# ReLUs and output sums of an MLP placed first by a planner, slack planned for attention and Fourier tasks, and weights loaded between the second batch's pairs

## The chip, the core and the metric

The kernel runs on one core of a Trainium2 chip. Five engines work side by side, each through its own instructions strictly in order: TensorE (PE in the profile; PEld is its weight load), VectorE (DVE), ScalarE (ACT), GpSimd (POOL) and SyncE (SP). SP, ACT and POOL also issue DMA transfers, which run on sixteen DMA engines. An instruction that waits holds up everything behind it on its engine. The metric is the device time of one execution in microseconds (us). The median of three runs of the kernel before is 344.29 us.

## What is computed

```python
def _attn_ref(q, k, v, mem_k, mem_v):            # q, k, v: 4 x 8 heads x 768 x 64
    chunk, left_ctx, right_ctx = (32, 16, 8)     # 8 memory rows per head
    for c in range(nc):
        k_full = concat(mem_k, k[l_start:r_end]); v_full = concat(mem_v, v[l_start:r_end])
        a = softmax(scale * q_c @ k_full.T)
        out[c] = a @ v_full

def _moe_ref(x, w_ch1, w_ch2):                   # x: 4 x 768 x 512, from the heads of out
    u = x + real(fft(fft(x, axis=1), axis=2))
    un = (u - mean(u)) / sqrt(var(u) + 1e-06)    # over the 512 columns
    return u + maximum(un @ w_ch1, 0.0) @ w_ch2  # w_ch1 512 x 2048, w_ch2 2048 x 512
```

All inputs and the output are float32.

## The kernel before

There are four batches. Each goes through three stages.

*Attention.* A batch has eight heads, handled as four pairs. The pairs are numbered 0 to 15 over all batches, so pairs 0 to 3 are batch 0 and pairs 4 to 7 batch 1. For one pair, SP loads Q, K and V (`e_load_q`, `e_load_k`, and `e_load_v` once for each head; tiles `qf`, `kf`, `va`, three buffers each, reused in turn). Q and K are cast to bf16 (`qb`, `kb`, one buffer each): on DVE for batch 0, on POOL for the others. PE turns them (`trq`, `trk`), ACT copies the turned tiles (`qT`, `kTb`). POOL copies a piece of each head's `va` to other partitions (`e_overlap`, L299). PE then makes scores for half of the sequence (`sc`, 12 matmuls), ACT takes the exponential (`e`), PE multiplies with the values (`xa`, 24 matmuls), and DVE divides (L373, L374) into the batch's `xsb`; all this twice a pair. `sc` and `xa` have one PSUM buffer each.

*Fourier part.* DVE folds `xsb` by symmetry (`zy`, `pq`, `ff`), and the result is split into a high and a low half-precision part (`hi` on ACT, `lo` on DVE). This is done for an even and an odd part, called parity 0 and parity 1 here. PE makes the transform along the sequence (`ps`, 60 matmuls a batch), ACT and DVE write it back (`up`, `dn`), PE makes the transform along the columns (`pm`, 48 matmuls a batch, in six column tiles of 8). For each tile DVE adds it into `xsb` and takes mean and variance (L474, L480, L481), ACT writes the centred row (`un`), PE turns it (`tp`), DVE copies it (`unT`). POOL makes one `rstd` a batch when all six tiles have their variance.

*MLP.* Two halves of the sequence. Each has 16 products `ph` of four matmuls (w1), each followed by a ReLU on ACT (`hT`), and then three output tiles `pc` of 16 matmuls (w2). DVE adds each output to `xsb` (`osb`, L534) and ACT issues the store.

*Weights.* `w1_sb` and `w2_sb` are each filled by four DMA transfers that POOL issues (L671, L673); they convert from float32 on the way.

*What sets the order.* All work is added as tasks to `Plan` (L38 to L113), each with an engine, a planned cost, tasks that it follows, buffers that it takes and gives, and a rank. `Plan.order` plays the tasks forward in planned time: whenever an engine is free it takes the task of lowest rank that is ready and finds its buffers free. On SP nothing may overtake: the lowest rank is waited for. The sequence that comes out is the program order of every engine; on the chip only dependencies count, and planned times have no other effect. A `margin` makes a task count as ready only so much after the task on another engine that it follows. Rank is normally the order of adding. MLP tasks have `MLPS` (1000000) added, so that they go after all attention and Fourier tasks that are ready. Tasks with `fill=True` are warming matmuls on zeros with the highest rank; the first `ph` ends them.

```python
mg, mgl = (MARGIN, 3 * MARGIN) if b == 1 else (0.0, 0.0)
...
add("PE", 0.28, lambda: e_warm(5), [t_warm], rank=2 * MLPS, fill=True)
```

Of the kernel before, what the change touches and what calls it, by code (L numbers as in the profile page):

```python
# [34 lines left out]
MARGIN = 0.5  # L35


class Plan:  # L38
# [18 lines left out]
    def order(self):  # L57
# [7 lines left out]
        placed = []  # L65
        while any(waiting.values()):
# [39 lines left out]
            if not moved:  # L106
                times = ([v for v in idle.values() if v > now] + [g[0] for g in gives]
                         + [x for t in placed for x in (t["done"], t["done"] + MARGIN, t["done"] + 3 * MARGIN) if x > now])
# [8 lines left out]
def kernel(  # L117
# [439 lines left out]
    for i in range(NKT):  # L557
        t_clear["kTb", i] = add("POOL", 1.15, lambda i=i: nc.gpsimd.memset(kTb[i], 0.0))
# [9 lines left out]
    for nm, parts, y, r, NN, c in (("S", tabS, yS.rearrange(fl3), rS.rearrange(fl3), S, 1.3),  # L568
                                   ("D", tabD, yD.rearrange(fl2), rD.rearrange(fl2), DM, 0.6)):

        t1 = [add("DVE", 0.5, lambda p_=p_: nc.vector.tensor_scalar(
# [13 lines left out]

    def attention(n):
        b, pr = seq[n]
        lq = add("SP", 0.35, lambda: e_load_q(n), take=("qf",), moved=1.3)
        lk = add("SP", 0.35, lambda: e_load_k(n), [t_clear["kf", n] if n < NS else None],
                 take=("kf",), moved=1.3)  # L590
        lv = [add("SP", 1.1, lambda hh=hh: e_load_v(n, hh),
                  [t_ones[n] if n < NV else None],
                  take=("va",) if hh == 0 else (), moved=1.2) for hh in range(2)]
        first = b == 0
        mg, mgl = (MARGIN, 3 * MARGIN) if b == 1 else (0.0, 0.0)
# [3 lines left out]
        ov = [add("POOL", 0.84, lambda hh=hh: e_overlap(n, hh), [lv[hh]], margin=mgl) for hh in range(2)]  # L599
        behind = kept.get("v0") if b == 1 else None  # L600
        tq = add("PE", 0.40, lambda: e_turn_q(n), [cq, t_idb, behind], take=("tr",), give=("qb",),
                 margin=mg)
# [4 lines left out]
                 margin=mg)  # L607
# [4 lines left out]
        for g in range(2):  # L612
            s_ = add("PE", 0.32, lambda g=g: e_scores(n, g), [eq, ek], take=("sc",),
                     give=("qT", "kTb") if g == 1 else (), margin=mg)
# [5 lines left out]
                     margin=mg)  # L620
# [40 lines left out]
    def e_all_sines():  # L661
# [9 lines left out]
    t_w1 = [add("POOL", 0.7, lambda dt=dt: nc.gpsimd.dma_start(  # L671
        w1_sb[:, dt, :], moe_w_ch1[ts(dt, P), :]), [x_last], moved=3.5) for dt in range(NDT)]
    t_w2 = [add("POOL", 0.7, lambda g=g: nc.gpsimd.dma_start(  # L673
        w2_sb[:, ts(g, 4), :], w2v[:, ts(g, 4), :]), [x_last], moved=3.5) for g in range(4)]


    def fourier(b):
        nrm = [[t_norm[b * HP + i, g] for i in ii for g in range(2)] for ii in ((0, 1), (2, 3))]
# [86 lines left out]

    def RELU(i):
        return MLPS + i
# [46 lines left out]
```

## Time and profile before

| what | value |
|---|---|
| median of three runs (lowest to highest) | 344.29 us (340.43 to 344.6) |
| the profiled execution: its time, its span | 341.38 us, 339.6 us |
| mean granted TensorE clock | 0.967 |
| PE busy | 311.2 us (92%) |
| DVE, ACT, POOL busy | 187.6, 168.3, 81.1 us |
| read from and written to HBM | 28.11 MB, 6.29 MB |

The span runs from the first to the last instruction; 1.8 us of the execution's own time lie outside it. Rows of a timeline give the start, the duration, the engine, the line, the operation, the output and input tiles and a count; a bracket at the end says how long the engine stood idle before the row and what ended that. Rows of the chain of waits give start, duration and a piece of the chain that ended last. In the strips of the page each digit is a tenth of the busy share in one of forty slices of 8.49 us. Matmuls overlap each other, so a group's mean duration is longer than the time from one matmul to the next.

### The profile page before, as it was taken

How to read it: one execution, taken by the hardware profiler on the slowest of the kernel's cores; microseconds unless marked ns; L12 is line 12 of the kernel's file. 1: busy time of each engine (PE TensorE's matmuls, PEld its weight loads, DVE VectorE, ACT ScalarE, POOL GpSimd, SP SyncE). 2: the span in 40 equal slices, each digit the busy share in tenths (PEclk: the TensorE clock that was granted, in tenths of full speed). 3: DMA queues.
4: the chain of work that ended last, by engine and by line, in shares of the span. 5: the costliest groups of instructions: out<-in, count | busy, mean ns of one | idle time of the engine just before them, and what ended most of it. 6: DMA issues, size and time to landing. Idle time of an engine off the chain costs nothing.

```text
span 339.6 us, 7885 instructions
## 1 busy us (share of the span) xinstructions
PE 311.2 (92%) x3339; PEld 210.4 (62%) x3339; DVE 187.6 (55%) x359; ACT 168.3 (50%) x297; POOL 81.1 (24%) x88
## 2 busy tenths in 40 slices
PE   7978976999979999589999997799999999999995
PEld 7867974988656577466665655555645454554542
DVE  8945696289299988988673369860710100101001
ACT  7754873456867466758523723356226053250620
POOL 5333992231975145720001200000010000000000
PEclk9997997799999999969999999799999999999998
DMA  5999999996555065620001200010010100201001
GB/s 137 213 198 181 210 205 234 209 208 128 144 147 147 10 169 131 164 63 0 2 31 65 52 2 1 31 64 0 29 67 0 64 31 0 94 0 62 33 31 62
DMA packets 41890, 30.71 MB, mean 90 GB/s; under 512 B 30080, under 2 KB 32128, under 8 KB 41856
## 3 DMA queue, kind: packets, MB, share of 16 engines
q1 hardware_dynamic: 35424, 19.67, 27.1%
q0 software_dynamic: 2688, 4.19, 6.8%
q10 hardware_dynamic: 3744, 6.36, 5.0%
q8 instruction: 26, 0.43, 0.6%
q14 instruction: 8, 0.07, 0.1%
HBM read 28.11 MB, written 6.29 MB: 101 GB/s over the span
## 4 chain that ended last, share of the span: by engine, by line
PE 73%; DVE 10%; DMA 10%; ACT 4%; SPq 1%; issue 1%; ACTq 0%; POOL 0%; POOLq 0%
PE pc L528 25%; PE ph L514 22%; DMA qf<-in_q_dram 8%; PE pm L468 6%; PE xa L363 6%; PE ps L436 5%; PE warm L386 4%; DMA va<-in_v_dram 2%; DVE ff L413 2%; DVE lo L426 2%; PE tp L493 2%; PE sc L342 1%; DVE pq L404 1%; DVE pq L403 1%; ACT va L235 1%; DVE zy L396 1%
## 5 line engine op out<-in xcount | busy, mean ns | idle before, releaser
L521 ACT ACTIVATE hT<-ph 128x384 f16<-128x384 f32 x128 | 61.1, 492 | 70.9 <-PE ph L514 70.5
L514 PE MATMUL ph<-unT,w_sb 128*128 128x384 f16 x512 | 92.5, 327 | 3.9 <-DVE osb L534 3.2
L528 PE MATMUL pc<-w_sb,hT 128*128 128x512 f16 x384 | 87.3, 379 | 0.0
L514 PEld LDWEIGHTS <-w_sb 128*128 128x128 f16 x512 | 48.4, 97 | 37.7 <-issue 8.6
L534 DVE SCALAR_TENSOR_TENSOR osb<-pc,rstd,xsb 128x512 f32<-128x512 f32 x24 | 17.9, 748 | 84.1 <-PE pc L528 84.1
L528 PEld LDWEIGHTS <-hT 128*128 128x128 f16 x384 | 36.8, 98 | 40.5 <-issue 0.4
L299 POOL COPY va<-va 32x780 f32<-32x780 f32 x32 | 31.9, 1008 | 47.0 <-DMA va<-in_v_dram 35.0
L350 ACT ACTIVATE e<-sc,mbias 128x384 f32<-128x384 f32 x64 | 33.7, 581 | 14.1 <-PE sc L342 13.6
L386 PE MATMUL warm<-zeros 128*128 128x128 bf16 x506 | 38.1, 237 | 1.0 <-DVE zero L208 1.0
L386 PEld LDWEIGHTS <-zeros 128*128 128x128 bf16 x506 | 33.5, 107 | 2.0 <-DVE zero L208 1.0
L363 PE MATMUL xa<-va,e 128*64 128x65 f32 x768 | 30.1, 229 | 2.2 <-DVE xsb L374 2.2
L363 PEld LDWEIGHTS xa<-va,e 128*64 128x64 f32 x768 | 25.6, 140 | 7.6 <-issue 6.0
L486 ACT ACTIVATE un<-xsb,mu_s 128x512 f16<-128x512 f32 x24 | 17.3, 720 | 22.9 <-DVE mu_s L481 19.2
L502 POOL TENSOR_SCALAR rstd<-mu_s 128x6 f32<-128x6 f32 x4 | 1.1, 285 | 99.6 <-DVE osb L534 88.3
L448 ACT CAST up<-ps 128x386 f16<-128x386 f32 x16 | 9.6, 602 | 23.4 <-PE ps L436 23.4
L295 POOL CAST kb<-kf 104x1024 bf16<-104x1024 f32 x12 | 17.4, 1446 | 12.6 <-PE trk L321 8.6
L421 ACT CAST hi<-ff 128x768 f16<-128x768 f32 x16 | 13.2, 832 | 12.8 <-DVE ff L413 12.6
L436 PE MATMUL ps<-cosS,hi 128*128 128x193 f16 (+1 forms) x72 | 15.8, 275 | 3.3 <-DVE ff L413 3.3
L474 DVE TENSOR_TENSOR xsb<-pm,xsb 128x512 f32<-128x512 f32 x24 | 16.2, 674 | 4.3 <-PE pm L468 4.0
L374 DVE TENSOR_TENSOR xsb<-xa,zs 128x384 f32<-128x384 f32 x32 | 17.8, 557 | 1.1
L498 DVE COPY unT<-tp 128x512 f16<-128x512 f16 x24 | 9.9, 419 | 15.1 <-PE ph L514 11.6
L436 PE MATMUL ps<-cosS,lo 128*128 128x193 f16 (+1 forms) x72 | 15.6, 274 | 2.4 <-DVE lo L426 2.4
(93 smaller groups left out, 380.8 us busy)
## 6 DMA issues: line engine op xcount, KB each, us to landing
qf<-in_q_dram SPq DMA_DIRECT2D x16, 384.0 KB
kf<-in_k_dram SPq DMA_DIRECT2D x16, 384.0 KB
out_dram<-osb ACTq DMA_DIRECT2D x24, 256.0 KB
va<-in_v_dram SPq DMA_DIRECT2D x32, 176.0 KB
w_sb<-in_moe_w_ch_dram POOLq DMA_DIRECT2D x8, 512.0 KB, 15.3
va<-in_mem_v_dram SPq DMA_DIRECT2D x32, 24.0 KB
va<-in_v_dram SPq DMA_DIRECT2D x16, 28.0 KB
va<-in_v_dram SPq DMA_DIRECT2D x16, 4.0 KB
```

The source lines that it names most:

```text
L295: eng.tensor_copy(kb_of[n].rearrange(cp_b), kf[n % NS].rearrange(cp_q, j=RB))
L299: nc.gpsimd.tensor_copy(v1[0:32, 1:NB, 0:D + 1], v1[96:128, 0:NT, 0:D + 1])
L350: nc.scalar.activation(e1[:, :, :, ts(half, 32)], sc[:, :, 0:6, ts(half, 32)], AFT.Exp, bias=mbias[:, half:half + 1], scale=1.0 / math.sqr ...
L363: nc.tensor.matmul(xa[64 * half:64 * half + 64, st, hh, 0:65], e1[:, hh, t6, :], v1[:, 6 * g + t6 + 1, 0:65], start=True, stop=True)
L374: nc.vector.tensor_tensor(xs[b][:, 3 * g:3 * g + 3, 2 * pr * D:(2 * pr + 2) * D] .rearrange("p s (h d) -> p s h d", h=2), xa[:, :, :, 0:D] ...
L386: nc.tensor.matmul(warm_of[0], zeros, zeros, start=True, stop=True)
L436: nc.tensor.matmul(out_[:, sp, :], part[:, ab, sp * 3 + st, c0:c1], tab[:, sp, st, :], start=(st == 0 and i == 0), stop=(st == 2 and i == 1))
L468: nc.tensor.matmul(pm[:, par, :], lhs, rhs[:, par, :], start=(im == 0), stop=(im == 3))
L514: nc.tensor.matmul(ph[:, 0:384], w1_sb[:, dt, ts(ht, P)], unT_of[b][:, dt, sh * 384:(sh + 1) * 384], start=(dt == 0), stop=(dt == NDT - 1))
L521: nc.scalar.activation(hT_of[b, sh][:, ht, :], ph_of.pop((b, sh, ht))[:, 0:384], AFT.Relu, bias=0.0, scale=-1.0)
L528: nc.tensor.matmul(pc_of[b, sh, stl], hT_of[b, sh][:, ht, ts(stl, P)], w2_sb[:, ht, :], start=(ht == 0), stop=(ht == NHT - 1))
L534: nc.vector.scalar_tensor_tensor(osb, pc_of.pop((b, sh, stl)), rstd_of[b][:, st:st + 1], xs[b][:, st, :], ALU.mult, ALU.add)
```

## The change

1. *MLP ranks.* ReLU tasks, output sums (`osb`) and output stores get `len(plan.tasks) - MLPS`: they now go before everything else that is ready on ACT and DVE. `ph` and `pc` on PE keep their rank.
2. *Slack.* `SPARE` gives three margins a batch (PE tasks; ACT and DVE tasks; tasks behind a load): none for batch 0, 1.5, 0.7 and 2.0 for batch 1, 1.0, 0.3 and 0.5 for batches 2 and 3. Fourier tasks get them too.
3. *Loads on SP.* New ranks put Q and K of pair n+1 ahead of V of pair n, and the planned issue and transfer costs are larger.
4. *Weights.* w1 is issued behind the V copies of pair 4, w2 behind those of pair 6 (`W1_AT`, `W2_AT`), instead of both once pair 3 has its exponentials.
5. *Warming.* A fill is 6 matmuls planned at 0.8 instead of 5 planned at 0.28. 450 fill matmuls become 234; the 56 at the start stay.
6. *Small.* The memsets of `kTb` clear 32 of every 96 columns, and the planned cost of one table operation on DVE is 0.8 instead of 0.5.

```diff
-        lq = add("SP", 0.35, lambda: e_load_q(n), take=("qf",), moved=1.3)
...
+        lq = add("SP", 0.45, lambda: e_load_q(n), take=("qf",), moved=1.5, rank=10 * n)
+        lk = add("SP", 0.4, lambda: e_load_k(n), [t_clear["kf", n] if n < NS else None],
+                 take=("kf",), moved=1.5, rank=10 * n + 1)
+        lv = [add("SP", 2.1 if hh == 0 else 1.4, lambda hh=hh: e_load_v(n, hh),
+                  [t_ones[n] if n < NV else None], rank=10 * n + 15 + hh,
+                  take=("va",) if hh == 0 else (), moved=1.6) for hh in range(2)]
...
-        mg, mgl = (MARGIN, 3 * MARGIN) if b == 1 else (0.0, 0.0)
+        mgp, mg, mgl = SPARE[b]
...
+    SPARE = [(0.0, 0.0, 0.0), (1.5, 0.7, 2.0)] + [(1.0, 0.3, 0.5)] * (B - 2)
...
+    def load_w1(after):
+        return [add("POOL", 0.7, lambda dt=dt: nc.gpsimd.dma_start(
+            w1_sb[:, dt, :], moe_w_ch1[ts(dt, P), :]), [after], moved=3.2, rank=-1)
+            for dt in range(NDT)]
...
     def fourier(b):
+        def add(engine, cost, emit, after=(), **more):
+            return plan.add(engine, cost, emit, after, margin=SPARE[b][0 if engine == "PE" else 1],
+                            **more)
...
-                                rank=RELU(len(plan.tasks))))
+                                rank=len(plan.tasks) - MLPS))
...
-                          rank=MLPS + len(plan.tasks))
+                          rank=len(plan.tasks) - MLPS)
...
+    W1_AT, W2_AT = (1, 0), (1, 2)
...
+            if (b, i) == W1_AT:
+                t_w1 = load_w1(kept["ov"])
+            if (b, i) == W2_AT:
+                t_w2 = load_w2(kept["ov"])
...
-        add("PE", 0.28, lambda: e_warm(5), [t_warm], rank=2 * MLPS, fill=True)
+        add("PE", 0.8, lambda: e_warm(6), [t_warm], rank=2 * MLPS, fill=True)
```

Three places show the moves. The first is POOL at the start of batch 1. `va` buffers 82, 83 and 84 belong to pairs 3, 4 and 5, and 82 then to pair 6; `kb<-kf_80` and `kb<-kf_81` are pairs 4 and 5, and `kf_79` is pair 6. Before:

```order
L291 CAST qb<-qf_77 96x2x8x64
L295 CAST kb<-kf_80 104x2x8x64
L299 COPY va_83<-va_83 32x12x65
L671 DMA w_sb<-in_moe_w_ch_dram 128x2048 x4
L673 DMA w_sb<-in_moe_w_ch_dram 128x4x512 x4
L299 COPY va_83<-va_83 32x12x65
L291 CAST qb<-qf_78 96x2x8x64
L295 CAST kb<-kf_81 104x2x8x64
```

And after, in the same place on POOL:

```order
L297 COPY va_83<-va_83 32x12x65 x2
L677 DMA w_sb<-in_moe_w_ch_dram 128x2048 x4
L293 CAST kb<-kf_81 104x2x8x64
L297 COPY va_84<-va_84 32x12x65
L289 CAST qb<-qf_76 96x2x8x64
L297 COPY va_84<-va_84 32x12x65
L293 CAST kb<-kf_79 104x2x8x64
L297 COPY va_82<-va_82 32x12x65
L289 CAST qb<-qf_77 96x2x8x64
L297 COPY va_82<-va_82 32x12x65
L682 DMA w_sb<-in_moe_w_ch_dram 128x4x512 x4
L293 CAST kb<-kf_80 104x2x8x64
```

The first four weight transfers moved behind both V copies of pair 4, and the other four behind both V copies of pair 6, ahead of the K cast of pair 7.

The second place is SP at pairs 3 and 4 (`va0` is pair 3's V, `va1` pair 4's; `qf1` and `kf1` are pair 4's Q and K, `qf2` and `kf2` pair 5's). Before:

```order
L280 DMA va0_82<-in_v_dram 64x11x64
L281 DMA va0_82<-in_mem_v_dram 8x12x64
L260 DMA qf1_77<-in_q_dram 96x2x512
L265 DMA kf1_80<-in_k_dram 96x2x512
L278 DMA va1_83<-in_v_dram 8x2x64
L279 DMA va1_83<-in_v_dram 56x2x64
```

And after, on SP:

```order
L278 DMA va0_82<-in_v_dram 64x11x64
L279 DMA va0_82<-in_mem_v_dram 8x12x64
L258 DMA qf2_78<-in_q_dram 96x2x512
L263 DMA kf2_81<-in_k_dram 96x2x512
L276 DMA va1_83<-in_v_dram 8x2x64
L277 DMA va1_83<-in_v_dram 56x2x64
```

Pair 4's V now stands behind pair 5's Q and K.

The third place is PE in the Fourier part of batch 3, where the `ps` matmuls of parity 0 end (the last ones write one row, 1x193). Before:

```order
L436 LDWEIGHTS lo_3500
L436 MATMUL ps_3535<-cosS_105,lo_3500 1x193
L436 LDWEIGHTS hi_3572
L436 MATMUL ps_3579<-cosS_105,hi_3572 128x193
L436 LDWEIGHTS lo_3573
L436 MATMUL ps_3579<-cosS_105,lo_3573 128x193
```

And after, on PE:

```order
L434 LDWEIGHTS hi_3314
L434 MATMUL ps_3371<-cosS_105,hi_3314 1x193
L434 LDWEIGHTS lo_3315
L434 MATMUL ps_3371<-cosS_105,lo_3315 1x193
L512 LDWEIGHTS w1_sb_110
L512 MATMUL ph_3399<-unT_2452,w1_sb_110 128x384
```

Parity 1 followed parity 0 at once; now 28 matmuls of `ph` stand between them.

More of the change, by code (lines that the diff above doesn't have):

```diff
@@ L65, in order @@
         placed = []
+        margins = {0.0} | {t["margin"] for t in self.tasks}
         while any(waiting.values()):
@@ L107, in order @@
                 times = ([v for v in idle.values() if v > now] + [g[0] for g in gives]
-                         + [x for t in placed for x in (t["done"], t["done"] + MARGIN, t["done"] + 3 * MARGIN) if x > now])
+                         + [x for t in placed for x in (t["done"] + m for m in margins) if x > now])
                 assert times, [(t["engine"], t["no"], t["take"]) for ts_ in waiting.values()
@@ L557 @@
     for i in range(NKT):
-        t_clear["kTb", i] = add("POOL", 1.15, lambda i=i: nc.gpsimd.memset(kTb[i], 0.0))
+        t_clear["kTb", i] = add("POOL", 0.5, lambda i=i: nc.gpsimd.memset(
+            kTb[i].rearrange("p (b c) -> p b c", b=NB)[:, :, 64:96], 0.0))
     t_col = add("DVE", 0.6, e_rows_of_ones, [t_id])
```

29 lines of the change are left out of this document (11 added, 18 removed).

## The prediction

> **What bounds the kernel now.** I read the page's strips first, then its groups, then the chain of waits in order of time, and last the timelines of PE, POOL and SP.
>
> ```profile
> span 339.6 us, 7885 instructions
> PE   7978976999979999589999997799999999999995
> PEclk9997997799999999969999999799999999999998
> DMA  5999999996555065620001200010010100201001
> L514 PE MATMUL ph<-unT,w_sb 128*128 128x384 f16 x512 | 92.5, 327 | 3.9 <-DVE osb L534 3.2
> L528 PE MATMUL pc<-w_sb,hT 128*128 128x512 f16 x384 | 87.3, 379 | 0.0
> ```
>
> Two stages show. For nine slices (to about 76 us) the DMA engines are full, and PE is filled up with warming matmuls. After that the DMA engines are mostly idle and PE is full, with weak slices. The boundary is the first `ph`, since only the MLP gives PE more work than the loads allow:
>
> ```profile
> 81.49 0.81 PE L514 MATMUL ph<-unT,w_sb 128*128 128x384 f16 x4
> ```
>
> PE's true work is priced from pieces of the chain at full clock, since group means overlap:
>
> ```profile
> 61.09 0.29 PE sc L342 x12
> 64.82 1.01 PE ps L436 x12
> 70.25 1.75 PE pm L468 x16
> 72.00 0.85 PE xa L363 x24
> 78.70 0.34 PE trq L305 x8
> 80.45 0.33 PE tp L493 x4
> 82.52 0.37 PE trk L321 x8
> 314.71 10.40 PE ph L514 x64
> 325.11 10.37 PE pc L528 x48
> 335.51 0.75 DVE osb L534
> ```
>
> A pair costs 0.34 + 0.37 + 2 x 0.29 + 2 x 0.85 = 3.0 us, four of them 12.0. The Fourier part of a batch is 5 x 1.01 + 3 x 1.75 + 6 x 0.33 = 12.3, its MLP 2 x (10.40 + 10.37) = 41.5. A batch is 65.8, all four 263.2 us.
>
> Ahead of its first `ph`, the program order of before has 8 `trq`, 7 `trk`, 14 `sc`, 13 `xa`, all `ps` and `pm` of batch 0 and 4 of its `tp`: 32.0 us of work, done in 81.5. So 231.2 us remain. From the last `pc` (335.5) to the end of the span are 4.1 us. 339.6 - 81.5 - 231.2 - 4.1 leaves **22.8 us that PE loses after the first `ph`**. Most of it stands where a batch's Fourier part begins:
>
> ```profile
> 100.17 0.92 PE L363 MATMUL xa<-va,e 128*64 128x65 f32 x24 [2.17 <-DVE xsb L374]
> 144.64 0.80 PE L514 MATMUL ph<-unT,w_sb 128*128 128x384 f16 x2 [2.65 <-DVE osb L534]
> 147.21 0.34 PE L436 MATMUL ps<-cosS,lo 128*128 128x193 f16 x1 [0.98 <-DVE lo L426]
> 213.68 0.26 PE L436 MATMUL ps<-cosS,hi 128*128 128x193 f16 x1 [3.25 <-DVE ff L413]
> 140.00:150.00 10.00, 6.19 (x59) 4.44 (x60) 9.97 (x13) 5.96 (x12) 4.55 (x4) 0.66 0.52 136
> 210.00:220.00 10.00, 6.01 (x39) 4.43 (x37) 8.50 (x17) 3.45 (x5) 0.00 (x0) 0.83 0.07 26
> ```
>
> These four waits are 9.05 us. In the two windows the granted clock (third number from the end) was 0.66 and 0.83, so at most 3.4 + 1.7 = 5.1 us went there. Some 8.6 us are small waits and switches of task.
>
> **The change, part by part.**
>
> *Weights.* What they do to the loads before:
>
> ```profile
> 32.49 0.84 SPq L260 DMA_DIRECT2D qf<-in_q_dram  x1
> 38.94 0.75 SPq L260 DMA_DIRECT2D qf<-in_q_dram  x1
> 40.26 4.46 SPq L265 DMA_DIRECT2D kf<-in_k_dram  x1
> 62.12 0.34 SPq L260 DMA_DIRECT2D qf<-in_q_dram  x1
> 38.48 3.04 POOL L673 DMA_DIRECT2D w_sb<-in_moe_w_ch_dram  x4
> 44.33 5.40 POOL L295 CAST kb<-kf 104x1024 bf16<-104x1024 f32 x1
> 68.66 0.83 POOL L299 COPY va<-va 32x780 f32<-32x780 f32 x1 [1.80 <-DMA va<-in_v_dram]
> ```
>
> Pair 5's loads take 6.45 us of SP (32.49 to 38.94). Pair 6's take 23.2, with single issues of 4.46 us, as the eight weight transfers run beside them: 16.7 us of delay, 8.4 for each four. Pair 6's V is complete at 68.66. In the changed order only w1 is ahead of it, but also pair 7's Q and K, half of 6.45: I estimate 68.7 - 8.4 + 3.2 = 63.5 us. Bounds are 60 (w1 all done before) and 72 (no relief).
>
> The first `ph` hangs on two chains. One is batch 0's Fourier part:
>
> ```profile
> 49.79 0.54 PE L321 MATMUL trk<-ident_b,kb 104*128 104x104 bf16 x8 [1.99 <-POOL kb L295]
> 59.73 0.51 PE L305 MATMUL trq<-ident_b,qb 96*128 96x96 bf16 x8 [3.29 <-POOL qb L291]
> 61.31 2.85 PE L386 MATMUL warm<-zeros 128*128 128x128 bf16 x25
> 70.09 0.38 PE L468 MATMUL pm<-cosD,up 128*128 128x256 f16 x2
> ```
>
> Here PE stands 3.29 us before pair 6's `trq`, because its Q comes late; the `ps` of parity 1 are queued behind it, and then 25 warming matmuls hold PE for 2.85 us more. In the changed order Q of pair 6 precedes pair 5's V and the weights, so it has landed. Pair 5's `trk` stays at about 49.8 (its cast of 5.40 us on POOL now follows w1's issue and overlaps the same DVE work). Behind it come 24 `ps`, `sc` and `xa`: 2.0 + 0.3 + 0.85, and the next `trq` starts at 53.5 to 55.5; I take 54.5. From `trq` to the first `pm` were 10.4 us, of which 2.85 was warming; 6 of those matmuls now cost 0.7. `pm` comes at 54.5 + 10.4 - 2.85 + 0.7 = 62.7. From `pm` to `ph` were 11.4 us, a DVE chain that is unchanged: **first `ph` at 74 us**.
>
> The other chain is new: pair 8's `trq` and `trk` stand ahead of the first `ph`, and their casts stand on POOL behind w2's issue.
>
> ```profile
> 71.69 1.04 POOL L295 CAST kb<-kf 104x1024 bf16<-104x1024 f32 x1 [0.32 <-DMA kf<-in_k_dram]
> ```
>
> 63.5 + 0.83 (V copy) + 3.04 (w2's issue) + 3 x 1.04 (casts) + 0.37 (`trk`) = 70.9 us, just under 74. If pair 8's K lands late under w2's transfers, this chain decides; by as much as pair 6 was held up, 8.4 us, it gives 79. w2 itself, 8.4 us from 67, is in long before the first `pc`, which has 64 `ph` (10.4 us) ahead of it.
>
> Ahead of the first `ph` are then 9 `trq`, 9 `trk`, 15 `sc`, 13 `xa`, `ps`, `pm` and 5 `tp`: 33.7 us. 229.5 us remain.
>
> *Slack and MLP ranks.* The wait for `osb` (2.65) goes, since `osb` is first on DVE and the ReLUs first on ACT; the ReLUs push casts and exponentials back by a half us each, which the new slack covers on paper. At batch 3, 28 `ph` (4.5 us) now lie between the two parities, where 3.25 was lost. At batch 2, some 28 us of other PE work stand between the last division and the first `ps`, and about 10 us of DVE work must fit there: 0.98 goes. At batch 1 the filler is 12.6 us for DVE work of about 10 with `osb` added, so I keep the 2.17. Of 9.05 us of waits I keep 2.2 and allow 1.0 for new ones; of the clock's 5.1, two; the small 8.6 fall to 6.3. That is 11.5 us. The bounds are 5 (only small switches) and 22.8 (nothing gained).
>
> *Loads reordered.* Each V lands one Q and K later, 3.2 us, with two pairs of Q and K in hand. Batch 0 is held by PE and ACT steps as much as by V, so nothing there. Queued behind SP's waits for a free Q buffer is now the V of the pair before: a rival below.
>
> *Memset, table cost.* POOL stands idle for 2.58 us after the memsets, so a shorter one gains nothing and one of equal length loses nothing:
>
> ```profile
> 8.42 2.37 POOL L299 COPY va<-va 32x780 f32<-32x780 f32 x2 [2.58 <-DMA va<-in_v_dram]
> ```
>
> *Fewer warming matmuls.* 216 fewer. They filled waits ahead of the first `ph`, except where they stood in the way (counted above). What their absence may cost is the clock:
>
> ```profile
> 33.03 1.85 PE L386 MATMUL warm<-zeros 128*128 128x128 bf16 x30
> 50.00:60.00 10.00, 6.71 (x95) 5.29 (x91) 6.56 (x12) 3.57 (x7) 3.10 (x3) 0.83 1.17 227
> 60.00:70.00 10.00, 10.00 (x169) 9.28 (x167) 4.10 (x10) 5.30 (x9) 2.70 (x3) 0.83 1.13 211
> ```
>
> Thirty at full clock took 1.85 us (62 ns each); 25 after the idle 3.29 us took 2.85 (114 ns), in a window with granted clock 0.83, as the one before it. So idle PE is followed by slow PE. The Trainium skill, "TensorE: Matmul & The Clock Gate", in the part on the HAM clock gate, says that PE falls to half rate after an idle window of about 3.4 us and needs as long a busy one to recover; by that rule, which the trace bears out, the change risks a cold PE. I take no cost beyond the 0.7 above, for the waits ahead of 74 us are for data; the upper end is the cold rival.
>
> **Sum.** 74 + 229.5 + 11.5 + 4.1 = 319.1 us span, and 1.8 outside it (341.38 - 339.6): 320.9 us against a profiled 341.38. The median of the runs, 344.29, is 0.85% above that execution, so the forecast on the median's scale is 323.6, said as 324.
>
> **Rivals** (times on the median's scale).
>
> *The DMA queue only moves its jam.* w2 now floods pair 8's Q and K, and the first `ph` stays at 81.5 us; slack still pays. 81.5 + 229.5 + 11.5 + 5.9 = 328.4, scaled 331. For it: 40.26 shows what weights do to K. Against: Q and K are now queued ahead.
>
> *Slack is planned, not real.* `ph` at 74, but 22.8 stays lost, since new waits replace old: 332.2, scaled 335. For it: the DVE row of 140 to 150 has 9.97 busy of 10, and DVE's work does not shrink.
>
> *Neither*, the change does not do what it says: 81.5 + 229.5 + 22.8 + 5.9 = 339.7, scaled 343.
>
> *Cold PE.* At 114 instead of 62 ns a matmul, the 19 us of PE work between 50 and 74 us (`ps` 5.1, `pm` 5.3, five `xa` 4.3, the small tasks some 4) cost 16 more, 3.4 of them paid already (two windows at 0.83): +12.6, 333.5, scaled 336. The Trainium skill's clock gate would do it this way.
>
> *V behind Q and K: slower.* Every V of pairs 4 to 15 comes 3.2 us later, and PE, strictly in order, stands that long at each `xa`: 12 x 3.2 = 38, 359 us, scaled 362. It makes the kernel over 2% slower once the wait exceeds 27 us in all, 2.3 a pair. For it:
>
> ```profile
> POOL va L299 <- DMA va<-in_v_dram: 35.0, 13, 9.6
> ```
>
> V is what POOL waits for most. Against: PE stood only once before `xa`, for 2.17, and by 90 us the DMA engines are half idle.
>
> **Chances.** Forecast 0.50; jam moves 0.13; slack unreal 0.13; neither 0.09; cold 0.07; slower 0.08. Faster by over 2% means under 337.4; about 2% is what can be told here, as the three runs spread over 1.2%. The first two count as faster, most of the third and half of the fourth: 0.76. Same 0.16, slower 0.08. The range begins at first `ph` 71 with 5 lost (71 + 229.5 + 5 + 5.9 = 311.4, scaled 314) and ends at 338, beyond the cold and slack rivals; outside are "neither", "slower" and a little below.
>
> **What would show it.** First `ph` near 74, and V copies of pair 6 near 63; no SP issue of 4 us between pair 5's and pair 6's Q; waits of PE after the first `ph` of 3 to 5 us in all, none for `osb`; the batch 3 `ps` without a wait. Wrong would be: POOL's casts of pairs 7 and 8 behind w2 later than 72 us with PE idle for them, waits at `xa` of over 2 us a pair, or a granted clock well under 0.9 after 80 us.

## The result, and the profile after

The kernel after the change takes 319.7 us (median; 317.68 to 320.28), the kernel before, run beside it, 344.09 us (340.43 to 344.6). The ratio is 0.930, with a 95% interval of 0.923 to 0.938: 7% faster. The profiled execution of after took 319.55 us with a span of 317.8 us.

The page of after, with the same five lines as shown of before (span; PE, its granted clock and the DMA engines in forty slices, now 7.95 us each; the two MLP groups):

```profile
span 317.8 us, 7448 instructions
PE   7697759899999999999999999999999999999994
PEclk9989796999999999999999999999999999999998
DMA  7999999999981695910130001000100100101001
L512 PE MATMUL ph<-unT,w_sb 128*128 128x384 f16 x512 | 92.1, 325 | 1.3 <-DVE osb L532 0.8
L526 PE MATMUL pc<-w_sb,hT 128*128 128x512 f16 x384 | 88.2, 379 | 0.0
```

From the ninth slice on PE is at 9 until the last, and its granted clock is at 0.9 or more from the eighth. The two groups of MLP matmuls are as long as before to about 1% (92.1 and 88.2 us against 92.5 and 87.3): the work didn't shrink, the gaps did. Ahead of that PE is less busy than before in most slices, as there are fewer warming matmuls.

The boundary, again the first `ph` (timeline of PE, after):

```profile
76.04 1.47 PE L512 MATMUL ph<-unT,w_sb 128*128 128x384 f16 x8
```

What PE waits for from there to the end, by the view of waits cut to that stretch (who waits and for whom: us in all, times, longest). First before, from 82 us:

```profile
PE ps L436 <- DVE ff L413: 3.3, 1, 3.3
PE ph L514 <- DVE osb L534: 3.2, 4, 2.7
PE ps L436 <- DVE lo L426: 2.6, 4, 1.0
PE xa L363 <- DVE xsb L374: 2.2, 1, 2.2
```

Then after, from 76 us, the whole answer:

```profile
PE xa L361 <- DVE xsb L372: 0.9, 2, 0.6
PE ph L512 <- DVE osb L532: 0.8, 4, 0.3
PE ph L512 <- ACT hT L519: 0.3, 1, 0.3
PE xa L361 <- POOL kb L293: 0.3, 1, 0.3
```

The waits for `ff` and `lo` are gone and those for `osb` and `xsb` are small; in all 13.2 us became 2.3.

By the prediction's own division of the span:

| | before | after |
|---|---|---|
| first `ph` at | 81.49 us | 76.04 us |
| PE's true work ahead of it (piece prices of the prediction) | 32.0 | 33.7 |
| true work left | 231.2 | 229.5 |
| lost after the first `ph` | 22.8 | 8.2 |
| behind the last `pc` | 4.1 | 4.1 |

So of 21.8 us of span, 7.2 come from the stage of loads (5.45 earlier, and 1.7 us more work done by then) and 14.6 from PE's losses behind it.

Twelve kernels were run to find which edit bought which part. Each was timed beside the kernel before on the same chip, and the ratios below are to that. For every kernel "first `ph`", "work ahead" and "lost" are worked out from its trace as in the table above; "waits" are the idle times of PE of 0.15 us or more behind the first `ph`.

### The profile page after: what moved, and what is told of

The parts are those of the page before. It is cut to its first block, busy times and chain, and to the rows that moved or that the text cites. A ratio compares the mean times of both kernels' runs of the same rounds, so it can differ in the third digit from the quotient of the medians.

```text
span 317.8 us, 7448 instructions
## 1 busy us (share of the span) xinstructions
PE 297.1 (94%) x3123; PEld 197.0 (62%) x3123; DVE 189.6 (60%) x359; ACT 167.0 (53%) x297; POOL 80.2 (25%) x88
## 4 chain that ended last, share of the span: by engine, by line
PE 68%; DVE 19%; DMA 6%; ACT 2%; SPq 1%; issue 1%; POOL 1%; ACTq 0%; POOLq 0%
PE ph L512 26%; PE pc L526 22%; PE pm L466 6%; PE xa L361 5%; PE ps L434 5%; DMA va<-in_v_dram 4%; DVE zy L394 3%; DVE ff L411 3%; DVE osb L532 2%; DMA qf<-in_q_dram 2%; DVE pq L402 2%; DVE lo L424 2%; PE tp L491 2%; DVE pq L401 2%; PE sc L340 1%; DVE xsb L372 1%
## 5 line engine op out<-in xcount | busy, mean ns | idle before, releaser
L512 PE MATMUL ph<-unT,w_sb 128*128 128x384 f16 x512 | 92.1, 325 | 1.3 <-DVE osb L532 0.8
L526 PE MATMUL pc<-w_sb,hT 128*128 128x512 f16 x384 | 88.2, 379 | 0.0
L297 POOL COPY va<-va 32x780 f32<-32x780 f32 x32 | 35.2, 1106 | 69.5 <-DMA va<-in_v_dram 39.7
L348 ACT ACTIVATE e<-sc,mbias 128x384 f32<-128x384 f32 x64 | 33.7, 580 | 17.8 <-PE sc L340 15.6
L361 PE MATMUL xa<-va,e 128*64 128x65 f32 x768 | 31.4, 231 | 6.8 <-POOL va L297 5.2
L361 PEld LDWEIGHTS xa<-va,e 128*64 128x64 f32 x768 | 26.6, 142 | 13.9 <-POOL va L297 6.0
L384 PE MATMUL warm<-zeros 128*128 128x128 bf16 x290 | 23.8, 240 | 1.0 <-DVE zero L206 1.0
L384 PEld LDWEIGHTS <-zeros 128*128 128x128 bf16 x290 | 20.1, 109 | 1.4 <-DVE zero L206 1.0
L371 DVE RECIPROCAL zs<-xa 128x6 f32<-128x6 f32 x32 | 6.0, 188 | 23.3 <-PE xa L361 23.3
L394 DVE TENSOR_TENSOR zy<-xsb 128x768 f32<-128x768 f32 x16 | 19.5, 1226 | 0.2
L424 DVE TENSOR_TENSOR lo<-ff,hi 128x768 f16<-128x768 f32 x16 | 16.6, 1050 | 0.8 <-ACT hi L419 0.8
L478 DVE BATCH_NORM_STATS2 st<-xsb 128x6 f32<-128x512 f32 x24 | 16.6, 693 | 0.7
L434 PE MATMUL ps<-cosS,hi 128*128 128x193 f16 (+1 forms) x72 | 14.4, 260 | 2.7 <-ACT hi L419 2.7
```

Source lines behind the costliest of these rows:

```text
L297: nc.gpsimd.tensor_copy(v1[0:32, 1:NB, 0:D + 1], v1[96:128, 0:NT, 0:D + 1])
L348: nc.scalar.activation(e1[:, :, :, ts(half, 32)], sc[:, :, 0:6, ts(half, 32)], AFT.Exp, bias=mbias[:, half:half + 1], scale=1.0 / math.sqr ...
L361: nc.tensor.matmul(xa[64 * half:64 * half + 64, st, hh, 0:65], e1[:, hh, t6, :], v1[:, 6 * g + t6 + 1, 0:65], start=True, stop=True)
L384: nc.tensor.matmul(warm_of[0], zeros, zeros, start=True, stop=True)
L394: nc.vector.tensor_tensor(zy_of[b, par][:, :, c0:c0 + P], xb[:, :, c0:c0 + P], xb[:, :, HD + c0:HD + c0 + P], ALU.add if par == 0 else ALU ...
L424: nc.vector.tensor_tensor(lo[:, ab].rearrange(fl), ff_of[b, par][:, ab].rearrange(fl), hi[:, ab].rearrange(fl), ALU.subtract)
```

## Experiments on the weights and the loads

**All weights early, planned anew.** The kernel after, but with both weights issued where before had them, behind pair 3's exponentials. The planner takes the loads into account, so the order of all engines changes too.

```diff
+    t_w1, t_w2 = load_w1(x_last), load_w2(x_last)
     done = {0: fourier(0)}
...
-            if (b, i) == W1_AT:
-                t_w1 = load_w1(kept["ov"])
-            if (b, i) == W2_AT:
-                t_w2 = load_w2(kept["ov"])
```

> The changed kernel with one part undone: all eight weight transfers are issued behind pair 3's exponentials again. Theory A (the weights flooded the loads of pairs 5 and 6, and their split made the first ph earlier): the first ph goes back from 76 to 81 or 82 us, V of pair 6 lands at 70 or later, and PE loses about 8 us afterwards as now; some 325 us. Theory B (Q and K ahead of V is what brought the first ph forward, the weights don't matter): first ph within 1.5 us of 76, 320 us. Theory C (nearly all came from slack and ranks): 320 to 322 us.

Measured: 333.96 us (332.21 to 334.56), ratio 0.972 [0.962, 0.982]. First `ph` at 86.29 with 31.6 us of work ahead of it, 10.5 lost. So the place of the weights matters: the first `ph` came even later than before's 81.49. To part the transfers from the planner, the next two keep an order word for word.

**Only the issue moved, early.** After's program order on every engine, except that the eight weight issues stand on POOL behind pair 3's V copies.

```diff
-        kept["ov"] = ov[-1]
+        kept["ov"] = kept["ov", n] = ov[-1]
...
+        behind_ov = {id(kept["ov", n]): ws for n, ws in {3: t_w1 + t_w2}.items()}
+        weights = {id(w) for w in t_w1 + t_w2}
         for t in plan.order():
+            if id(t) in weights:
+                continue
             t["emit"]()
+            for w in behind_ov.get(id(t), ()):
+                w["emit"]()
```

> The changed kernel's program order on every engine, word for word, except that all eight weight transfers are issued behind the V copies of pair 3 on POOL, near 35 us. Theory A (contention of the transfers): the first ph goes from 76 to 84 to 87 us, as where the planner was told of early weights (86.3), the loss afterwards stays at 8 to 11 us, 328 to 332 us. Theory P (the transfers don't matter, the planner's order around them does): first ph within 2 us of 76 and 319 to 322 us.

Measured: 328.77 us (328.0 to 329.43), ratio 0.963 [0.956, 0.971]. The timelines of this kernel, PE at pair 6's `trq`, the first `pm` and the first `ph`, then POOL ahead of that `trq`:

```profile
59.32 0.82 PE L303 MATMUL trq<-ident_b,qb 96*128 96x96 bf16 x8 [4.64 <-POOL qb L289]
71.07 0.38 PE L466 MATMUL pm<-cosD,up 128*128 128x256 f16 x2
84.66 1.47 PE L512 MATMUL ph<-unT,w_sb 128*128 128x384 f16 x8
57.33 0.83 POOL L297 COPY va<-va 32x780 f32<-32x780 f32 x1 [10.85 <-DMA va<-in_v_dram]
58.23 1.03 POOL L289 CAST qb<-qf 96x1024 bf16<-96x1024 f32 x1
```

and PE's first two of these rows in after (the third is shown above):

```profile
54.79 0.52 PE L303 MATMUL trq<-ident_b,qb 96*128 96x96 bf16 x8
62.76 0.38 PE L466 MATMUL pm<-cosD,up 128*128 128x256 f16 x2
```

With the order unchanged, PE stands 4.64 us for the cast of pair 6's Q, and `pm` and `ph` come 8.3 and 8.6 us later. It isn't Q itself that is late now, as it was in before: SP issues it at 34.60, ahead of the jam. Its cast stands on POOL behind the copy of pair 5's V (the first of the two POOL rows), and that waits 10.85 us for its load; in after the same copy goes at 47.91 and the cast at 49.42. The loss behind the first `ph` is 8.0, as after's 8.2. So 8.6 us hang on the place of the eight issues alone, and all of it ahead of the first `ph`. Against this kernel the one above is another 1.6 us later with 2.1 us less work done, and loses 2.5 us more: about 6 us of its span come with the order that the planner makes when the weights are early.

**Only the issue moved, late.** The converse: before's order word for word, with w1 behind pair 4's V copies and w2 behind pair 6's.

```diff
+        kept["ov", n] = ov[-1]
...
+        behind_ov = {id(kept["ov", n]): ws for n, ws in {4: t_w1, 6: t_w2}.items()}
```

(and the same loop as above).

> The program order of the kernel before on every engine, word for word, except that w1 is issued behind both V copies of pair 4 and w2 behind those of pair 6. Theory A: pair 6's trq comes forward from 59.7 to about 55, the first ph from 81.5 to 74 to 77 us, the 22.8 us lost afterwards stay; 336 to 340 us. Theory P (only a new order can use the earlier loads): first ph at 80 to 82, 342 to 345 us.

Measured: 337.41 us (335.49 to 338.8), ratio 0.987 [0.975, 0.9996]. The timeline of PE of this kernel, at the same places, and a wait at batch 3:

```profile
55.27 0.51 PE L305 MATMUL trq<-ident_b,qb 96*128 96x96 bf16 x8
76.00 0.81 PE L514 MATMUL ph<-unT,w_sb 128*128 128x384 f16 x4
210.17 0.34 PE L436 MATMUL ps<-cosS,hi 128*128 128x193 f16 x1 [3.25 <-DVE ff L413]
```

The wait of 3.29 us before pair 6's `trq` is gone and the first `ph` stands at 76.00, 5.5 us earlier than before: the move alone does that. Behind it nothing improves: the wait of 3.25 us for `ff` is there, and 25.6 us are lost, 2.8 more than in before. Only 0.6 of that are waits; the granted clock is below full for longer (0.89, 0.60, 0.97 and 0.69 in the windows of 10 us from 130, 140, 200 and 210 us: at most 8.5 us in all, against 5.1 in before). So half of the early gain is lost again, and the span falls by 2.7 us. The median falls by 5.5 us, with an interval that only just leaves out no gain.

**V ahead of the next pair's Q and K.** The kernel after with the SP ranks taken out (the larger planned costs stay).

```diff
-        lq = add("SP", 0.45, lambda: e_load_q(n), take=("qf",), moved=1.5, rank=10 * n)
+        lq = add("SP", 0.45, lambda: e_load_q(n), take=("qf",), moved=1.5)
...
-                  take=("kf",), moved=1.5, rank=10 * n + 1)
+                  take=("kf",), moved=1.5)
...
-                  [t_ones[n] if n < NV else None], rank=10 * n + 15 + hh,
+                  [t_ones[n] if n < NV else None],
```

> The changed kernel with one part undone: on SP, V of a pair stands ahead of the next pair's Q and K again (larger planned costs kept). Theory A: pair 6's Q now queues behind pair 5's V under w1's transfers, trq of pair 6 comes at 57 to 60 instead of 54.8 us, first ph 2 to 4 us later, 322 to 324 us. Theory B (this part carries the earlier start): first ph at 81 or later, 325 us or more. If V behind Q and K was a cost, as the slower rival said: 318 us or less.

Measured: 320.51 us (319.39 to 321.83), ratio 0.934 [0.926, 0.942], not to be told from after. The parts differ and cancel: first `ph` at 72.34 with 31.6 us of work ahead (3.7 earlier with 2.1 less done), then 11.8 lost against 8.2. So the rival by which Q and K ahead of V cost 3.2 us at every pair is wrong: no such cost shows, and no gain in the sum either.

## Experiments on the slack and the MLP's ranks

**Old margins.**

```diff
-    SPARE = [(0.0, 0.0, 0.0), (1.5, 0.7, 2.0)] + [(1.0, 0.3, 0.5)] * (B - 2)
+    SPARE = [(0.0, 0.0, 0.0), (0.5, 0.5, 1.5)] + [(0.0, 0.0, 0.0)] * (B - 2)
...
-            return plan.add(engine, cost, emit, after, margin=SPARE[b][0 if engine == "PE" else 1],
+            return plan.add(engine, cost, emit, after, margin=0.0,
```

> The changed kernel with one part undone: the margins are those of before (0.5 and 1.5 for attention of batch 1 alone, none for Fourier tasks). Theory A (slack removes the waits at the starts of Fourier parts): first ph at 76 to 79, then 15 to 20 us lost on PE instead of 8, with waits for DVE of 1 to 3 us at ps of batches 1 to 3; 328 to 333 us. Rival (the MLP ranks removed those waits, slack is unreal): 320 to 322 us.

Measured: 332.19 us (331.52 to 335.36), ratio 0.970 [0.961, 0.979]. PE's timeline, the two largest waits and the first `ph`:

```profile
66.96 0.87 PE L319 MATMUL trk<-ident_b,kb 104*128 104x104 bf16 x8 [6.58 <-POOL kb L293]
83.45 0.81 PE L512 MATMUL ph<-unT,w_sb 128*128 128x384 f16 x4
150.37 0.26 PE L434 MATMUL ps<-cosS,lo 128*128 128x193 f16 x1 [3.04 <-DVE lo L424]
```

and POOL's timeline of the same kernel ahead of the first of them:

```profile
62.81 3.01 POOL L682 DMA_DIRECT2D w_sb<-in_moe_w_ch_dram  x4
65.86 1.04 POOL L293 CAST kb<-kf 104x1024 bf16<-104x1024 f32 x1
```

Here the planner had put a `trk` and, behind it, all `pm` of batch 0 where it believed `kb` to be ready. On the chip POOL reached that cast only behind w2's issue (62.81, 3.01 us), which itself follows V's copies, and PE stood 6.58 us in front of `trk` with the `pm` queued behind. That puts the first `ph` at 83.45, 7.4 us later than in after (0.5 us more work done). Behind it 13.2 us are lost instead of 8.2, with the old kind of wait for `lo`. So planned slack is worth about 12 us here, and more than half of it ahead of the first `ph`, where the expectation had placed almost none: in after the `pm` begin at 62.76 (row above), ahead of that `trk`. That the larger margin for tasks behind a load is the one of the three that does it was not tried.

**Old MLP ranks.** ReLUs, output sums and stores last again, everything else as in after.

```diff
-                                rank=len(plan.tasks) - MLPS))
+                                rank=MLPS + len(plan.tasks)))
```

(and the same for output sums and stores).

> The changed kernel with one part undone: ReLUs, output sums and stores have the high rank of before on ACT and DVE. Theory A (slack did most): one wait for osb of 2 to 3 us comes back and little else, 322 to 324 us. Rival (ranks did most): 10 or more us more lost after the first ph, 330 us or more.

Measured: 335.9 us (334.38 to 336.09), ratio 0.978 [0.970, 0.986]. First `ph` at 77.49, near after's, but 23.0 us lost, as much as before's 22.8. The ranks cost the most of the three parts, though the intervals overlap, and all but 1.5 us of it lies behind the first `ph`. Two more runs part the two kinds of task.

**Only the ReLUs first.**

```diff
-                          rank=len(plan.tasks) - MLPS)
+                          rank=MLPS + len(plan.tasks))
...
-                    rank=len(plan.tasks) - MLPS)
+                    rank=MLPS + len(plan.tasks))
```

(the two tasks are `osb` and the store).

> The changed kernel with only the ReLUs placed first on ACT; output sums and stores have the high rank of before. The run without all MLP ranks lost 23.0 us after its first ph, this change's own kernel 8.2. If the ReLUs did it (PE waited for ACT in ph): 9 to 12 us lost, 320 to 324 us. If the output sums did it (a PSUM buffer of pc is held until osb has run): 18 us or more lost, 330 us or more, with waits for osb.

Measured: 333.59 us (332.08 to 334.52), ratio 0.974 [0.969, 0.979]; first `ph` at 76.0 as in after, 20.8 lost.

**Only the output sums and stores first.**

```diff
-                                rank=len(plan.tasks) - MLPS))
+                                rank=MLPS + len(plan.tasks)))
```

(the task is the ReLU).

> The changed kernel with only output sums and stores placed first; ReLUs have the high rank of before. If the output sums did it: 9 to 12 us lost, 320 to 324 us. If the ReLUs did it: 18 us or more lost, 330 us or more, with waits of PE for hT. If it takes both, each of the two runs comes out near 328.

Measured: 323.21 us (322.19 to 323.81), ratio 0.944 [0.940, 0.949]; first `ph` at 77.27, 9.6 lost.

So the output sums with their stores carry it: from the ratios, 0.044 (some 15 us) come back with them, and 0.014 (some 5 us, the intervals just apart) with the ReLUs.

How an addition on DVE can cost that much is in the traces. `pc` and `ph` share two PSUM buffers (the tile pool has `mlp=2`), and a `pc` buffer comes free only by its `osb`. For the kernel with only the ReLUs first, the view of the tile `pc` (count, shortest/median/longest ns, first and last start) and PE's timeline:

```profile
L526 PE MATMUL pc<-w_sb,hT x384: 376/379/390, 90.7 to 325.8; 128*128 128x512 f16 x192
L532 DVE SCALAR_TENSOR_TENSOR osb<-pc,rstd,xsb x24: 731/751/752, 120.1 to 326.3; 128x512 f32<-128x512 f32 x24
108.30 0.92 PE L361 MATMUL xa<-va,e 128*64 128x65 f32 x24 [1.97 <-DVE xsb L372]
120.90 1.02 PE L526 MATMUL pc<-w_sb,hT 128*128 128x512 f16 x4 [0.87 <-DVE osb L532]
```

and the same view of after:

```profile
L526 PE MATMUL pc<-w_sb,hT x384: 376/379/390, 90.7 to 313.3; 128*128 128x512 f16 x192
L532 DVE SCALAR_TENSOR_TENSOR osb<-pc,rstd,xsb x24: 732/751/752, 98.3 to 313.7; 128x512 f32<-128x512 f32 x24
```

Both begin `pc` at 90.7. In after the first `osb` runs at 98.3; with the old rank it stands on DVE behind the attention and Fourier work of batch 1 until 120.1. The first two `pc` tiles then hold both buffers: the second is done at 104.7, no MLP matmul goes until 120.90, and PE has only tasks of which several themselves wait for DVE. No store stands ahead of this first sum, so here it is the sum's own rank. The windows of the stretch from 105 to 121 us (PE's busy time first; granted clock third from the end), ReLUs only first, then after:

```profile
105.00:121.00 16.00, 11.32 (x174) 9.52 (x172) 14.82 (x27) 6.65 (x11) 4.86 (x4) 0.89 0.16 37
```

```profile
105.00:121.00 16.00, 15.12 (x202) 11.06 (x201) 15.86 (x26) 8.68 (x16) 6.06 (x6) 1.00 0.69 167
```

PE is busy 11.32 us of 16 in the one and 15.12 in the other, while DVE is nearly full in both. The same again at batch 3, in milder form. PE and then DVE, ReLUs only first:

```profile
209.86 0.81 PE L512 MATMUL ph<-unT,w_sb 128*128 128x384 f16 x4 [0.64 <-ACT hT L519]
211.25 0.81 PE L512 MATMUL ph<-unT,w_sb 128*128 128x384 f16 x4 [0.58 <-ACT hT L519]
...
217.35 3.59 PE L512 MATMUL ph<-unT,w_sb 128*128 128x384 f16 x20
```

```profile
214.22 0.74 DVE L532 SCALAR_TENSOR_TENSOR osb<-pc,rstd,xsb 128x512 f32<-128x512 f32 x1
```

The half's last `pc` was done before the first of these `ph`, its `osb` runs at 214.22. In between one buffer is left for `ph`, and with matmul and ReLU in turn there is a product every 1.39 us; once `osb` is through, five run in 3.59 us without a wait (the last row). The waits of 0.15 us or more sum to 11.55 us in this kernel against 2.32 in after, 9.2 of the 12.6 us of lost time between them; the rest is spread over pieces too small to name. Of the 9.2, 2.3 are one wait of a `trq` (at 131.84) for a cast of Q on POOL, which the run with only the sums first has too (2.4) and after hasn't; they are not the sums' work.

**The ranks alone.** The kernel before with only the three ranks changed.

```diff
-                                rank=RELU(len(plan.tasks))))
+                                rank=len(plan.tasks) - MLPS))
...
-                          rank=MLPS + len(plan.tasks))
+                          rank=len(plan.tasks) - MLPS)
...
-                    rank=MLPS + len(plan.tasks))
+                    rank=len(plan.tasks) - MLPS)
```

> The kernel before with nothing but the MLP ranks changed (ReLUs, output sums, stores first). If ranks work by themselves: the first ph stays at 81 to 82 us, and 10 to 14 us are lost afterwards instead of 22.8; 331 to 336 us. If they need slack in the plan to work: 18 us or more lost, 339 to 344 us.

Measured: 329.79 us (328.43 to 330.49), ratio 0.963 [0.958, 0.968]: 13.0 us from three ranks. Lost time is 11.3 instead of 22.8, and the first `ph` at 80.09 is 1.4 us earlier than before's with the same work ahead. What is left of the two largest waits (view of waits from 76 us):

```profile
PE ps L436 <- DVE lo L426: 3.7, 3, 2.4
PE xa L363 <- DVE xsb L374: 1.5, 1, 1.5
```

Here are the waits that slack was to remove, for `lo` and `xsb`; after has 0.9 us of them, all for `xsb`.

## Experiments on the warming matmuls

**No fills.** After without its 234 fill matmuls; the 56 at the start stay.

```diff
-    for i in range(300):
+    for i in range(0):
```

> The changed kernel without any warming fill (the 56 at the start stay). The fills also occupy PE in the planner's time, so the order shifts a little. Theory A (fills hide nothing by now): granted clock of 0.8 and less up to 70 us, first ph at 75 to 79 us, 318 to 323 us. Cold theory (idle PE goes to half clock and the work ahead of the first ph costs up to 12 us more): first ph at 82 or later, 327 us or more.

Measured: 326.67 us (324.74 to 327.61), ratio 0.957 [0.947, 0.966]; first `ph` at 81.69 with 34.9 us of work ahead, 8.8 lost. Two windows of this kernel and, second, one of after:

```profile
30.00:40.00 10.00, 5.83 (x92) 4.97 (x86) 4.47 (x17) 7.23 (x11) 3.57 (x5) 0.53 1.08 207
40.00:50.00 10.00, 3.56 (x39) 2.69 (x39) 9.90 (x10) 5.62 (x8) 9.71 (x10) 0.50 1.16 192
```

```profile
40.00:50.00 10.00, 6.58 (x93) 5.90 (x91) 9.96 (x18) 5.69 (x8) 9.83 (x9) 0.81 1.11 205
```

The granted clock falls to 0.53 and 0.50 without fills, where after has 0.81; the first `ph` comes 5.7 us later with 1.2 us more work done, and the time is 7 us longer. Cold PE is a likely cause, but the planner's order differs without fills as well, and no run parts the two. The 0.81 is a mean: in windows of 1 us the clock of after is 1.00 from 40 to 46 us, 0.50 from 47 to 53, with PE busy, and 1.00 from 53 on. So after's fills keep PE from being cold for long, not from being cold at all. The Trainium skill, "TensorE: Matmul & The Clock Gate", Part 1, says that the gate knows only half and full rate and falls to half after an idle window of about 3.4 us. The two rates agree with these windows; the length does not, as PE's longest idle time is 2.69 us in after and 2.43 us in the kernel without fills.

**The old fills.** After with the fills of before, 5 matmuls planned at 0.28 (520 of them in this order).

```diff
-        add("PE", 0.8, lambda: e_warm(6), [t_warm], rank=2 * MLPS, fill=True)
+        add("PE", 0.28, lambda: e_warm(5), [t_warm], rank=2 * MLPS, fill=True)
```

> The changed kernel with the fills of before: 5 matmuls planned at 0.28. Theory A (fills stand in the way of data that has come): some 200 more warming matmuls, first ph 1 to 4 us later than 76, 321 to 324 us. Cold theory: a warmer PE ahead of the first ph, clock near 1.0 from 30 to 70 us, first ph at 74 or earlier, 317 to 319 us.

Measured: 321.99 us (321.45 to 322.54), ratio 0.944 [0.936, 0.951], not clearly apart from after's 0.930 [0.923, 0.938]. The same window:

```profile
40.00:50.00 10.00, 8.69 (x161) 8.34 (x158) 9.90 (x10) 5.65 (x7) 9.70 (x10) 1.00 1.13 187
```

The clock is full and PE busier, and yet the first `pm` is at 62.81 (62.76 in after) and the first `ph` at 74.36 with 31.9 us of work ahead: 1.7 us earlier with 1.8 less done, and 10.7 lost. So a gain from 1.00 instead of 0.81 in this stage does not show. Even a low clock there need not cost: the kernel with V first has 0.55 in the same window and the earliest first `ph` of all, 72.34. The orders of these kernels differ, so the clock's own share stays open.

## A mixture

**V first in batch 0 only.** Of the two SP orders, V ahead of the next Q and K gave the earlier first `ph`, Q and K ahead the smaller loss behind it. This kernel takes the first order for pairs 0 to 3 and the second for the rest.

```diff
-                  [t_ones[n] if n < NV else None], rank=10 * n + 15 + hh,
+                  [t_ones[n] if n < NV else None], rank=10 * n + (15 if n >= HP else 5) + hh,
```

> A mix to beat both: the changed kernel with V ahead of the next pair's Q and K in batch 0 alone. The run that had it so for all batches reached its first ph at 72.3 us with 31.6 us of work done (the changed kernel 76.0 with 33.7, so 1.6 us behind), but lost 11.8 us afterwards instead of 8.2. From the second batch on the order is now that of the changed kernel. If the early gain adds to its small loss: first ph at 72 to 73, 8 to 9 us lost, 317.5 to 319 us. If the early gain is given back: 319 to 321 us.

Measured: 318.0 us (316.88 to 318.34, six runs), ratio 0.929 [0.925, 0.933]. First `ph` at 73.44 with 31.6 ahead, 7.0 lost. It is the lowest median of all, 1.7 us below after's, but the two ratios' intervals overlap: whether it beats after is open.

The runs together (not all were timed side by side, so the ratios are what compares):

| kernel | median us | ratio [95%] | first `ph` | work ahead | lost |
|---|---|---|---|---|---|
| before | 344.09 | 1 | 81.49 | 32.0 | 22.8 |
| after | 319.7 | 0.930 [0.923, 0.938] | 76.04 | 33.7 | 8.2 |
| weights early, planned anew | 333.96 | 0.972 [0.962, 0.982] | 86.29 | 31.6 | 10.5 |
| weights early, order kept | 328.77 | 0.963 [0.956, 0.971] | 84.66 | 33.7 | 8.0 |
| before, weights late | 337.41 | 0.987 [0.975, 0.9996] | 76.00 | 32.0 | 25.6 |
| V first | 320.51 | 0.934 [0.926, 0.942] | 72.34 | 31.6 | 11.8 |
| old margins | 332.19 | 0.970 [0.961, 0.979] | 83.45 | 34.2 | 13.2 |
| old MLP ranks | 335.9 | 0.978 [0.970, 0.986] | 77.49 | 33.7 | 23.0 |
| ReLUs only first | 333.59 | 0.974 [0.969, 0.979] | 76.0 | 33.7 | 20.8 |
| output sums only first | 323.21 | 0.944 [0.940, 0.949] | 77.27 | 33.7 | 9.6 |
| before, MLP ranks | 329.79 | 0.963 [0.958, 0.968] | 80.09 | 32.0 | 11.3 |
| no fills | 326.67 | 0.957 [0.947, 0.966] | 81.69 | 34.9 | 8.8 |
| old fills | 321.99 | 0.944 [0.936, 0.951] | 74.36 | 31.9 | 10.7 |
| V first in batch 0 | 318.0 | 0.929 [0.925, 0.933] | 73.44 | 31.6 | 7.0 |

The parts don't add. Taken out one at a time, weights, slack and ranks cost 0.042, 0.040 and 0.048 of the ratio, 0.130 in all, where the whole change brought 0.070. Two of them alone on before bring 0.013 (weights, order kept) and 0.037 (ranks). This fits parts that remove some of the same waits, but no run takes two of them out together.

## Why the prediction was right

The forecast was 324 us with a range of 314 to 338, and a chance of 0.76 for faster by over 2%. The time is 319.7, and it is faster. The case that the prediction held likeliest is the one that came, though not every step of its working.

*The sum.* Of its four terms, the work left (229.5) and the tail (4.1) held as they stood. The first `ph` was put 2.0 us too early (74 against 76.04), and the loss behind it 3.3 us too high (11.5 against 8.2); the two errors partly cancel, for a span of 317.8 us against 319.1. The other 2.7 us of the forecast came from scaling the profiled execution up to the median (0.85%): after's profiled execution of 319.55 us lies at its median.

*Weights.* Right in the main: moving the issues behind those loads is what brings the first `ph` forward. After's POOL and PE, at pair 6 and, in the last two rows, pair 8:

```profile
63.99 0.83 POOL L297 COPY va<-va 32x780 f32<-32x780 f32 x1
64.77 3.01 POOL L682 DMA_DIRECT2D w_sb<-in_moe_w_ch_dram  x4
71.68 1.04 POOL L293 CAST kb<-kf 104x1024 bf16<-104x1024 f32 x1 [1.84 <-issue]
75.66 0.54 PE L319 MATMUL trk<-ident_b,kb 104*128 104x104 bf16 x8
```

Pair 6's V copy at 63.99 was forecast for 63.5, its `trq` (54.79) for 54.5 and the first `pm` (62.76) for 62.7. The `trq` came so close partly by luck: pair 5's `trk` went at 48.77, 1.0 us ahead of its forecast, and from there to `trq` took 6.0 us instead of 4.7, with the granted clock at 0.50 until 53. The reason given for it, that Q of pair 6 "has landed", was half of it: with the issues moved back Q is as early, and its cast waits for pair 5's V all the same. The step that missed is the last, "from `pm` to `ph` were 11.4 us, a DVE chain that is unchanged": it took 13.3, as one more `trq`, `sc`, `xa` and `tp` and two `trk` now stand between them (0.34 + 0.29 + 0.85 + 0.33 + 2 x 0.37 = 2.6 us by the prediction's pieces, with 22 warming matmuls fewer), on a PE that is busy for 13.06 of these 13.28 us. The prediction counted that work (33.7 us ahead instead of 32.0) but did not put it into this step. The second chain, over the casts behind w2, was forecast for 70.9 and would have been through at 73.1: pair 8's K is cast at 71.68 (1.04 us), and its `trk` takes 0.37. That `trk` goes only at 75.66, with PE busy since the cast, so this chain did not decide. The run with only the issue moved back (8.6 us) shows the whole effect; the rival "the queue only moves its jam" has fallen.

*One sign was badly chosen.* "No SP issue of 4 us between pair 5's and pair 6's Q" came true, but could not have failed: before had none there either, its jam stood between pair 6's Q (38.94) and pair 7's (62.12). In after the jam stands between pair 7's and pair 8's, in SP's timeline:

```profile
42.21 0.40 SPq L258 DMA_DIRECT2D qf<-in_q_dram  x1
48.94 8.00 SPq L279 DMA_DIRECT2D va<-in_mem_v_dram  x1
57.04 0.40 SPq L258 DMA_DIRECT2D qf<-in_q_dram  x1
```

From Q to Q are 14.83 us, 8.4 more than pair 5's loads of before took (6.45): the price of "8.4 for each four" weight transfers. That it agrees to the tenth is luck, as the time from Q to Q varies by more than that from pair to pair. w1's transfers (issued on POOL at 44.17) hold up pair 6's V and pair 8's Q; pairs 6 and 7 have their Q and K ahead of that. The relief comes from what now stands in front of the jam, not from the jam's going.

*Slack and ranks.* The total was near (11.5 forecast, 8.2 measured), the sharing out was wrong. The step "the wait for `osb` (2.65) goes, since `osb` is first on DVE" gives the ranks one wait's worth and puts the other gains on the slack. The runs show the ranks at some 13 us alone on before and 16 in after, and in after most of it hangs on the output sum's rank. The prediction read the wait for `osb` where it was written in the trace, as 3.2 us in all. It missed that a late `osb` also holds the buffers which let MLP matmuls fill PE while DVE works. That cost carries other names in the trace: with the ranks alone on before, not only the waits for `osb` shrank (from 3.2 to 0.6), the 3.3 us for `ff` went too (those for `lo` grew from 2.6 to 3.7). So the total came near though its parts were put down to the wrong edit, which is in part luck. Slack was given only losses behind the first `ph`; it is worth 5.0 us there and 7.4 ahead of it.

*What was forecast to stay or to go.* Waits behind the first `ph`: 3.2 forecast, 2.32 measured; the sign "3 to 5 us in all, none for `osb`" missed a little on both counts, as 0.8 of them are for `osb`. At batch 1 the 2.17 for `xsb` was to stay; it is 0.65:

```profile
108.34 0.92 PE L361 MATMUL xa<-va,e 128*64 128x65 f32 x24 [0.65 <-DVE xsb L372]
```

The cost of the clock was to fall from 5.1 to 2 and is nothing that shows (granted clock 1.00 in every window of 10 us from 60 to 310 us). The small switches are 5.9 against 6.3 forecast. The `ps` of batch 3 go without a wait, as forecast.

*Rivals.* "Slack is planned, not real" (335) is wrong: without the slack the kernel takes 332.19 us, with it 319.7. "Cold PE" did not come as priced: after's clock is at 0.50 for some 6.8 us from 46 to 53 us, where the prediction took no cost, and `pm` is on time even so. Without fills PE is cold for longer and the time 326.67, in another order. The prediction's "which the trace bears out" holds for slow PE behind idle time, and not for the quoted length of 3.4 us: PE's longest idle time in before is the 3.29 us that the prediction showed. "V behind Q and K" has fallen with the run that undoes it.

## What to carry to other kernels

A task that gives back a scarce buffer belongs first on its engine, even where the trace shows little direct waiting for it: what it holds up appears elsewhere, as waits of the work that is left to fill the gap. Where instruction order is planned from costs, slack is worth planning, since one late task at the head of an engine's queue stops everything behind it (6.58 us here); which tasks need it most was not tried. Large transfers with a late deadline belong behind the loads that are due sooner. To part such edits, keep the program order word for word and move one thing, for a planner that plans anew moves several.

## What the runs showed of the hardware that was not expected

A single DMA issue on SP can hold SP for 8.00 us while weight transfers run (row at 48.94 above), where one of the same kind takes 0.73 us ahead of them, in the same timeline:

```profile
38.67 0.73 SPq L279 DMA_DIRECT2D va<-in_mem_v_dram  x1
```

In after it fell on memory rows of 24 KB; in the kernel with the weights early and the order kept, the longest fell on a V of 176 KB:

```profile
41.99 6.41 SPq L278 DMA_DIRECT2D va<-in_v_dram  x1
```

So it isn't one transfer's own size. Which issue is held, and by what, no run here shows.

A mean granted clock of 0.81 in the stage of loads cost nothing that shows against 1.00 (first `pm` at 62.76 and 62.81), and 0.55 went with the earliest first `ph`; without any fills, at 0.50 to 0.53 from 30 to 50 us, the first `ph` came 5.7 us later. These kernels differ in their order too. The clock fell to 0.50 though PE was never idle for longer than 2.69 us in after.
